# Eight of sixteen layer norms moved from VectorE to GpSimd in a linear-attention block

## The chip, the cores and the metric

The kernel runs on one core of a Trainium2 chip. The metric is the time on the device in microseconds (us). Each kernel is executed several times, and one execution is recorded by the hardware profiler; durations, waits and idle times come from that one.

## What is computed

The input x has 2048 tokens of 640 features in bf16. Each token is normalised (layer norm without weights), and the result xn feeds two branches whose product is added to x.

```python
xn = (x - mean(x)) / sqrt(var(x) + 1e-5)
q, k, v = split(xn @ wqkv)                # 32 heads of 20
phi = lambda t: where(t > 0, t + 1, exp(t)) + 1e-6
kv  = phi(k)^T v                          # per head, over all 2048 tokens
z   = sum over tokens of phi(k)
s   = (phi(q) kv / (phi(q) z + 1e-6)) @ wo
g   = silu(relu(xn @ w1) @ w2)            # w1: 640 x 1728, w2: 1728 x 640
out = x + s * g
```

## The kernel before

The 2048 tokens are 16 token tiles of 128 (tile t; tokens on the 128 partitions, 640 columns), in four chunks j of 512 tokens. Most products are done as pairs of chunks or tiles in a seven-product scheme in place of eight (the units a, b, p, q, m, u, o, g with steps s1 to s7): some products of a unit take sums or differences of operands, which VectorE forms in SBUF, and VectorE and ScalarE combine and evacuate the PSUM banks.

**Layer norm of a tile.** `LN_stats(t)` gives VectorE two BATCH_NORM_STATS (L630) and one BATCH_NORM_AGGREGATE (L634), then GpSimd two one-column instructions: L636 adds epsilon to the variance (`rsv`), L638 raises it to the power -0.5 (`rsy`), the reciprocal deviation. `LN_norm(t)` (L649) is one instruction on 128 x 640 bf16 that subtracts the mean and multiplies by `rsy`, both per-partition scalars, and writes `xn`. Behind it `xnT_dma(t)` (L698) issues on SP a transposing DMA from `xn` to `xnT`, which TensorE reads. Tiles 0 to 3 also have a short way at the start, in which only the mean is taken off first.

**What reads it.** The high tiles, 8 to 15, are read transposed by the K halves (`K_mm`, L709; Ka9 is the first 320 columns of tile 9, Kb8 the second of tile 8), by hh1 = `H_half(1)` (narrow matmuls, L817, all of tiles 8 to 15; hh0 in front of it takes tiles 0 to 7), by T1 = `h_T` (VectorE subtractions for the b units), and by the units themselves (L1198). The sum over tokens of phi(k) is done by accumulating DMAs issued by GpSimd (`z_put`, L897, words y0 to y15); the first of each of its two chains waits for the transposes of all tiles 8 to 15.

**What sets the order.** A class `Sched` records every operation with its reads and writes. `PROGRAM` is a text of words written out by hand (n8 is statistics and norm of tile 8, in which the statistics of tile 8 have been done earlier; the others up to n15 do both). TensorE and SP run their operations in the order in which they were recorded. VectorE, ScalarE and GpSimd are reordered after the first part (`end_of_head`): `place` plays the program with costs from `cost`, and for each of these engines picks among the next 60 operations the one that can start first, with ties going to the one that is due first (`late`, counted back from TensorE's queue). Waits on semaphores are then put in by `emit`. Each engine executes its own list strictly in order.

On SP the norms' transposes stand in the order n8, n9, n11, n10, n14, n12, n15, n13, with loads of x and w1 between them. In `PROGRAM` the part around the last two is

```
... n12 p1.s3 n15 p1.s4 p0.s1 Ka8 p0.s5 a0.s5 p0.s6 a0.s1 p0.s2 Kb11 a0.s6 p0.s7 p0.s3 n13
Ka10 Ka11 a0.s3 p0.s4 a0.s7 a0.s2 Kb9 Ka14 a3.s1 a0.s4 a2.s5 Kb12 a3.s5 a3.s6 a2.s1 hh0 hh1 ...
```

Other lines that matter: L735 and L737 finish phi(k) on VectorE (`K_fin`), L782 and L970 finish phi(q) (`f_sum`); L970 is the helper `tt` for all two-input adds and subtractions of VectorE, with both inputs in SBUF or one in PSUM; L1082 (`scale_rows`) is a GpSimd cast of 128 x 512; L1482 is ScalarE's evacuation of a K half.

Of the kernel before, what the change touches and what calls it, by code (L numbers as in the profile page):

```python
# [4 lines left out]
ALU = mybir.AluOpType  # L5
# [27 lines left out]
def _cols(ap):  # L33
    n = 1
    for d in ap.shape[1:]:
        n *= d
    return n


def _wide(ap):  # L40
    return str(ap.dtype).endswith("float32")


def cost(E, fn):
    seen = _Seen()
    fn(seen)
    name, a, k = seen.call
    aps = [v for v in list(a) + list(k.values()) if hasattr(v, "shape") and hasattr(v, "dtype")]
    if E == "PE":
        if name == "transpose":  # L50
            return (0.107, 0.107) if a[1].offset % a[1].ap[0][0] < 640 else (0.056, 0.107)
        n = _cols(k["rhs"]) / 2400.0
        part = k["lhsT"].shape[-1] / 128.0 if k.get("tile_position") is not None else 1.0
        return max(n * part + 0.0025, 0.026), n
    n = max(_cols(v) for v in aps)
    if E == "ACT":
        more = 0.19 if k.get("accum_out") is not None else 0.0
        if n > 512:
            more += 0.02
        if n == 1 and k["func"] == ACTF.Silu:  # L60
            more += 1.3
        if hasattr(k.get("scale"), "shape"):
            more += 0.08
        if _wide(k["out"]) and _wide(k["in_"]) and k["out"].tensor.name == k["in_"].tensor.name:
            return 0.05 + 0.0009 * n, 0.17 + 0.00083 * n
        return 0.05 + 0.00083 * n + more, 0.17 + 0.00083 * n + more
    if E == "POOL":
        return (0.66, 0.66) if k.get("op") is ALU.pow else (0.33 + 0.0025 * n, 0.33 + 0.0025 * n) if n > 12 else (0.33, 0.33)
    out = k["out"] if "out" in k else a[0]
    wide = any(_wide(v) for v in aps if _cols(v) > 4)  # L70
    if name == "bn_stats":
        return 0.403, 0.478
    if n <= 12:
        return 0.13, 0.21
    if name == "reciprocal":
        return 0.815, 0.9
    if name in ("tensor_copy", "tensor_scalar", "memset"):
        more = 0.06 * sum(hasattr(k.get(q), "shape") for q in ("scalar1", "scalar2"))
        return (0.065 + 0.00105 * n, 0.15 + 0.00105 * n) if wide else (0.08 + 0.00024 * n + more, 0.16 + 0.00025 * n + more)
    if wide or name != "tensor_tensor":  # L80
        return 0.064 + 0.00105 * n, 0.155 + 0.00105 * n
    return 0.075 + 0.000515 * n, 0.148 + 0.00052 * n
# [12 lines left out]
class Sched:  # L95
# [44 lines left out]
    def _record(self, E, kind, fns, R, W, extra, sem=None):  # L140
# [5 lines left out]
        if kind == "dma":  # L146
            seen = _Seen()
            fns[0](seen)
            name, a, _k = seen.call
            o.turn = "transpose" in name  # L150
            o.occ = 1.3 if o.turn else 1.25 if E == "POOL" else 0.5
            fat = a[1].tensor.name
            if fat in ("in_A_wo_dram", "reg3") and E == "SP" and not o.turn:
                o.occ = 0.65
            size = 2.0
            for d in a[0].shape:
                size *= d
            names = [v.tensor.name for v in a[0:2]]
            o.byt = 0.6 if o.turn else size / {"scr": 205e3}.get(names[0], {"scr": 240e3}.get(names[1], 310e3))
            lag = 0.5 if names[1] == "scr" else 0.8 if names[1] == "reg3" and names[0] == "reg6" else 0.0  # L160
            if o.turn and names[0] == "wv_sb":
                o.byt = 2.0
            o.dur = 4.6 if E == "POOL" else 2.1 + o.byt if o.turn else 1.95 + o.byt + lag
        else:
            o.occ, o.dur = 0.0, 0.0
            o.turn = E == "PE" and any(_narrow(fn) for fn in fns)
            for fn in fns:
                occ, dur = cost(E, fn)
                o.dur = o.occ + dur
                o.occ += occ  # L170
# [178 lines left out]
def bass_recurrent_scan__linear_attn_block__dense_activation_relu__prompt_kernel(  # L349
# [159 lines left out]
    sc = Sched(nc, NDS)  # L509
# [20 lines left out]
    def xs(t):  # L530
        return t if t < XR else (t - 4) % XR
# [112 lines left out]
        aggr(t)  # L644

    norms = []

    def LN_norm(t):
        norms.append(sc.op("DVE", lambda eng: eng.tensor_scalar(  # L649
            out=xn[:, t, :], in0=xin[:, xs(t), :], scalar1=mv[:, t, 0:1], scalar2=rsy[:, t:t + 1],  # L650
            op0=ALU.subtract, op1=ALU.mult), R=[("xin", xs(t)), ("mv", t), ("rsy", t)], W=[("xn", t)]))
        xnT_dma(t)
# [44 lines left out]
    def xnT_dma(t):  # L697
        dma("SP", lambda eng: eng.dma_start_transpose(  # L698
            xnT[:, t // 4, :, P * (t % 4):P * (t % 4 + 1)], xn[:, t, :]), R=[("xn", t)], W=[("xnT", t)])
# [667 lines left out]
    def run(ops):  # L1367
        for op_ in ops:
            op_[0](*op_[1:])

    S, N, F, SH, ZS, T0 = LN_stats, LN_norm, K_fin, h_S, scale_h, h_T
    after = [[(S, 5), (N, 4)], [(S, 6), (N, 5)], [(S, 7), (N, 6)], [(F, 0), (N, 7)], [(F, 1)]]
    for n, f in enumerate(HP):
# [576 lines left out]
```

## Time and profile before

| | |
|---|---|
| median of 3 runs | 203.54 us (203.54 to 203.79) |
| the profiled execution | 203.94 us, of which 202.7 us are the span from first to last instruction |
| busy, share of the span | TensorE 98%, VectorE 85%, ScalarE 63%, GpSimd 18% |
| chain that ended last | PE 82%, DMA 11%, issue 3%, DVE 3% |
| GpSimd L636 (1 column) x16 | 4.1 us, mean 259 ns |
| GpSimd L638 (1 column) x16 | 9.7 us, mean 608 ns |
| VectorE L649 (640 columns) x16 | 393 to 447 ns |

In the profile TensorE is PE (its weight loads PEld), VectorE is DVE, ScalarE ACT, GpSimd POOL, SyncE SP. A digit of the slices is the busy share of a fortieth of the span in tenths. In a timeline a row gives start, duration, engine, line, operation, output <- input, shapes and count, and in brackets how long the engine had been idle in front of it and what released it. Consecutive instructions of VectorE and ScalarE overlap by some 0.1 us in the records, so that the distance of starts is less than the duration.

### The profile page before, as it was taken

The page shows a single profiled execution, that of the slowest core. Times are in us where ns is not written, and L with a number is a line of the kernel's source. Part 1 is how long each engine was busy: PE and PEld are TensorE (multiplying, and loading weights), DVE is VectorE, ACT ScalarE, POOL GpSimd, SP SyncE. Part 2 cuts the span into 40 slices and gives each one's busy share as a digit, 9 for nine tenths or more (in the row PEclk, how much of TensorE's full clock was granted, in tenths as well). Part 3 has the DMA queues.
Part 4 walks back from the last instruction along what each step waited for, and adds up shares of the span by engine and source line. Part 5 has one row for each costly group of instructions (what it writes and reads, how often), then busy time and mean ns, then how long its engine had stood idle before and what let it go on. Part 6 is the DMA issues. An engine that isn't in the chain of part 4 may idle for free.

```text
span 202.7 us, 3677 instructions
## 1 busy us (share of the span) xinstructions
PE 198.6 (98%) x1334; PEld 123.8 (61%) x1344; DVE 172.2 (85%) x404; ACT 128.5 (63%) x268; POOL 37.2 (18%) x66
## 2 busy tenths in 40 slices
PE   8999999999999999999999999999999999999995
PEld 7755644545444454445645778777777777777773
DVE  4898999999997678899988879999978896855765
ACT  6497959799988486999662132463544645563452
POOL 3183051332256436422200000000000000000000
DMA  6976995662359858963462799338961106106103
GB/s 194 330 210 126 261 205 111 141 143 44 68 131 178 172 108 162 226 129 65 96 167 56 241 293 315 117 98 256 366 209 65 66 32 165 65 26 173 65 16 113
DMA packets 38328, 30.43 MB, mean 150 GB/s; under 512 B 13478, under 2 KB 38310, under 8 KB 38310
## 3 DMA queue, kind: packets, MB, share of 16 engines
q1 hardware_dynamic: 32437, 23.24, 41.0%
q0 software_dynamic: 4624, 5.57, 14.0%
q10 hardware_dynamic: 1248, 1.39, 2.1%
q8 instruction: 10, 0.16, 0.3%
q14 instruction: 9, 0.07, 0.1%
HBM read 15.81 MB, written 5.24 MB: 104 GB/s over the span
## 4 chain that ended last, share of the span: by engine, by line
PE 82%; DMA 11%; issue 3%; DVE 3%; ACT 0%; POOLq 0%; DVEq 0%
PE psT L1025 42%; PE psT L1198 18%; PE psT L709 10%; DMA regH<-reg 6%; PE psT L799 5%; DMA regH<-regH 3%; DMA reg<-in_A_x_dram 1%; PE psT L817 1%; PE psT L761 1%; PE psT L1826 1%; PE psT L682 1%; PE psT L1621 1%; PE psT L1595 1%; DVE regH L970 1%; PE psT L929 1%
## 5 line engine op out<-in xcount | busy, mean ns | idle before, releaser
L1198 PE MATMUL psT<-reg 128*128 128x512 bf16 (+1 forms) x135 | 36.8, 379 | 0.5 <-DVE regH L970 0.2
L1025 PE MATMUL psT<-reg,regH 128*128 128x320 bf16 (+1 forms) x224 | 35.0, 299 | 0.0
L1025 PE MATMUL psT<-reg 128*128 128x320 bf16 (+1 forms) x178 | 28.6, 299 | 0.0
L1025 PEld LDWEIGHTS psT<-reg,regH 128*128 128x128 bf16 (+1 forms) x224 | 21.9, 98 | 8.5
L1198 PEld LDWEIGHTS psT<-reg 128*128 128x128 bf16 (+1 forms) x141 | 13.4, 98 | 16.6 <-DVE regH L970 1.1
L897 POOL DMA_DIRECT2D regH<-reg x16 | 18.4, 1206 | 24.7 <-DMA regH<-reg 8.7
L1032 ACT ACTIVATE reg<-psT 128x320 f32<-128x320 f32 (+1 forms) x24 | 10.4, 435 | 17.8 <-PE psT L1025 15.9
L1025 PEld LDWEIGHTS psT<-reg 128*128 128x128 f16 (+1 forms) x178 | 17.4, 98 | 6.9
L970 DVE TENSOR_TENSOR reg<-reg 128x1024 f16<-128x1024 bf16 (+9 forms) x28 | 18.7, 673 | 1.1 <-PE psT L1025 1.0
L709 PE MATMUL psT<-reg 128*128 128x320 bf16 x120 | 18.7, 299 | 0.0
L1248 ACT ACTIVATE regH<-psT 128x512 bf16<-128x512 f32 (+1 forms) x24 | 15.2, 644 | 2.5 <-PE psT L1198 2.1
L1025 PE MATMUL psT<-reg,pqT 128*128 128x320 bf16 (+1 forms) x84 | 16.6, 299 | 0.0
L970 DVE TENSOR_TENSOR psT<-psT,reg 128x320 f32<-128x320 f32 (+1 forms) x21 | 11.4, 543 | 5.7 <-PE psT L1025 3.9
L1652 ACT ACTIVATE wv_sb<-psT 128x320 bf16<-128x320 f32 x22 | 9.6, 437 | 10.3 <-PE psT L1025 10.2
L709 PEld LDWEIGHTS psT<-reg 128*128 128x128 bf16 x120 | 11.7, 98 | 7.0
L1482 ACT ACTIVATE regE<-psT 128x320 bf16<-128x320 f32 x32 | 13.8, 538 | 2.9 <-PE psT L709 2.8
L630 DVE BATCH_NORM_STATS2 stats<-reg 128x6 f32<-128x320 bf16 x32 | 14.1, 473 | 1.3 <-DMA reg<-in_A_x_dram 1.3
L1032 ACT ACTIVATE psT<-psT 128x320 f32<-128x320 f32 x17 | 7.2, 426 | 10.3 <-PE psT L1025 10.3
L970 DVE TENSOR_TENSOR reg<-psT,reg 128x320 bf16<-128x320 f32 (+2 forms) x17 | 8.4, 499 | 4.2 <-PE psT L1025 4.1
L1841 ACT ACTIVATE reg<-psT 128x640 bf16<-128x640 f32 (+1 forms) x14 | 7.9, 569 | 5.1 <-PE psT L1025 5.1
L778 ACT ACTIVATE pqT<-psT 128x512 bf16<-128x512 f32 x16 | 10.6, 669 | 0.0
L776 ACT ACTIVATE regE<-psT 128x512 bf16<-128x512 f32 x16 | 10.1, 664 | 0.7 <-PE psT L761 0.5
(164 smaller groups left out, 385.5 us busy)
## 6 DMA issues: line engine op xcount, KB each, us to landing
regH<-reg POOLq DMA_DIRECT2D x16, 320.0 KB, 3.8
reg<-in_B_w_dram SPq DMA_DIRECT2D x12, 320.0 KB, 4.7
scr<-rden SPq DMA_DIRECT2D x4, 640.0 KB, 6.2
reg<-in_A_x_dram SPq DMA_DIRECT2D x4, 640.0 KB, 8.8
out_dram<-reg SPq DMA_DIRECT2D x14, 160.0 KB, 1.8
regE<-scr SPq DMA_DIRECT2D x3, 640.0 KB, 4.7
reg<-in_A_x_dram SPq DMA_DIRECT2D x4, 320.0 KB, 3.5
reg<-in_A_wo_dram SPq DMA_DIRECT2D x6, 160.0 KB, 5.2
```

The source lines that it names most:

```text
L630: sc.op("DVE", lambda eng: eng.bn_stats(stats[:, t, a, :], xv[:, HN * a:HN * (a + 1)]), R=[("xin", xs(t))], W=[("stats", t, a)])
L709: fns.append(lambda eng, a=a, k=k, lhs=lhs: eng.matmul(ps[bk[a]][:, 0:HN], lhsT=lhs, rhs=wk[:, k, HN * a:HN * (a + 1)], start=(k == 0), st ...
L776: exps.append(sc.op("ACT", lambda eng: eng.activation(out=e_, in_=src, func=ACTF.Exp), R=[key], W=[("er_e", es)]))
L778: sc.op("ACT", lambda eng: eng.activation(out=pqT[:, f, schunk(j)], in_=src, func=ACTF.Relu), R=[key], W=[("pqT", j, f)], extra=hz(gone))
L799: sc.group("PE", [(lambda eng, k=k: eng.matmul(ps[b], lhsT=w1_col(k, P * f, P), rhs=src[:, k, :], start=(k == 0), stop=(k == C - 1))) for ...
L897: dma("POOL", lambda eng: eng.dma_start(zacc[a], src, **kw), R=[key] + after, W=[("zacc", a)], chain=zchain[a])
L970: sc.op("DVE", lambda eng: eng.tensor_tensor(out=out, in0=in0, in1=in1, op=op), R=R, W=W, extra=extra)
L1025: sc.group("PE", [(lambda eng, k=k, lhs=lhs, rhs=rhs: eng.matmul(ps[b][:, 0:HN], lhsT=lhs, rhs=rhs, start=(start and k == 0), stop=(k == n ...
L1032: sc.op("ACT", lambda eng: eng.activation(out=dst, in_=ps[b][:, 0:HN], func=ACTF.Copy), R=[("ps", b)], W=[dkey], extra=extra)
L1198: sc.group("PE", [(lambda eng, k=k, lhs=lhs, rhs=rhs: eng.matmul(ps[b][:, 0:nn], lhsT=lhs if tile is None else rhs, rhs=rhs if tile is Non ...
L1248: sc.op("ACT", lambda eng: eng.activation(out=dst, in_=ps[b], func=ACTF.Relu), R=[("ps", b)], W=[("hT", j, f)], extra=ex)
L1482: sc.op("ACT", lambda eng, func=func, slot=slot: eng.activation(out=ek[:, eks(t), slot, HN * a:HN * (a + 1)], in_=ps[b][:, 0:HN], func=fun ...
```

## The change

The norms of tiles 8 to 15 are given to GpSimd, where their `rsv` and `rsy` are also done. The planner's cost of a GpSimd instruction with more than 12 columns is set from 0.33 + 0.0025 n to 0.33 + 0.0016 n us. PROGRAM, and with it the orders of TensorE and SP, stay; the orders of VectorE, ScalarE and GpSimd are worked out anew by `place`.

```diff
     if E == "POOL":
-        return (0.66, 0.66) if k.get("op") is ALU.pow else (0.33 + 0.0025 * n, 0.33 + 0.0025 * n) if n > 12 else (0.33, 0.33)
+        return (0.66, 0.66) if k.get("op") is ALU.pow else (0.33 + 0.0016 * n, 0.33 + 0.0016 * n) if n > 12 else (0.33, 0.33)
...
     norms = []
+    NP = range(8, 16)
 
     def LN_norm(t):
-        norms.append(sc.op("DVE", lambda eng: eng.tensor_scalar(
+        norms.append(sc.op("POOL" if t in NP else "DVE", lambda eng: eng.tensor_scalar(
             out=xn[:, t, :], in0=xin[:, xs(t), :], scalar1=mv[:, t, 0:1], scalar2=rsy[:, t:t + 1],
             op0=ALU.subtract, op1=ALU.mult), R=[("xin", xs(t)), ("mv", t), ("rsy", t)], W=[("xn", t)]))
         xnT_dma(t)
```

## The prediction

> **What bounds the kernel now.** I read the page first (busy shares, the 40 slices, the chain), then the stretches from 24 us on, then the line of the norms, and last the timeline in order of time around the GpSimd work and around the last norm.
>
> ```profile
> PE 198.6 (98%) x1334; PEld 123.8 (61%) x1344; DVE 172.2 (85%) x404; ACT 128.5 (63%) x268; POOL 37.2 (18%) x66
> ...
> DVE  4898999999997678899988879999978896855765
> ACT  6497959799988486999662132463544645563452
> POOL 3183051332256436422200000000000000000000
> ```
>
> TensorE has work in 98% of the span, so the end is set by its queue, which is in a fixed order, and by whatever makes that queue wait. The stretches show how dense it is where the eight norms lie (their VectorE starts are 26.82 to 51.34 us):
>
> ```profile
> 24.00:34.00 10.00, 10.00 (x49) 4.65 (x49) 9.54 (x25) 7.70 (x15) 4.23 (x11) 1.00 0.87 176
> 34.00:44.00 10.00, 9.95 (x53) 4.98 (x53) 9.69 (x29) 8.75 (x20) 3.24 (x8) 1.00 0.69 149
> 44.00:54.00 10.00, 9.95 (x56) 5.42 (x56) 9.99 (x31) 10.00 (x26) 1.64 (x4) 1.00 0.33 65
> 54.00:64.00 10.00, 9.89 (x77) 4.53 (x78) 9.72 (x27) 8.64 (x18) 5.09 (x5) 1.00 0.64 134
> ```
>
> After the length come TensorE, weight loads, VectorE, ScalarE, GpSimd, clock, DMA. From 24 to 64 us TensorE idles 0.21 us, from 24 to 200 us 0.61 us (175.39 busy of 176). A 512-column matmul is recorded 0.38 us long but the next starts 0.216 us later, so short gaps are hidden; by the spacing of the starts I count about 1.0 us of waiting in all after 24 us (the largest 0.34 us at 104 us). The granted clock is 1.00 throughout. VectorE is full too from 24 to 64 us, but TensorE hardly waits for it: its results come early enough. So a VectorE relief can win about 1 us at the very most, and a new wait of TensorE is lost in full, because nothing behind it has slack to give back.
>
> **What is removed: 8 norms on VectorE.**
>
> ```profile
> L649 DVE TENSOR_SCALAR reg<-reg,mv,rsy x16: 393/434/447, 13.4 to 51.3; 128x640 bf16<-128x640 bf16 x16
> ```
>
> Recorded 0.43 us, but pipelined: 31.59 to the next start 31.94 is 0.35 us. Eight of them give back 8 x 0.35 = 2.8 us of VectorE between 26.8 and 51.8 us. By itself this is worth nothing on TensorE, whose waits there sum to 0.2 us.
>
> **What is added: 8 norms on GpSimd.** No GpSimd row has 640 columns. The nearest ones: the same kind of instruction on one column (L636) takes 0.22 us; affine_select on 160 columns (L606) 0.35; the cast L1082 on 512 columns 0.85. From one column to the cast is (0.85 - 0.22) / 511 = 1.23 ns a column, so 640 columns come to 0.22 + 0.79 = 1.0 us. But look at what stood beside that cast:
>
> ```profile
> 25.41 0.32 DVE L735 TENSOR_SCALAR regE<-regE 128x640 bf16<-128x640 bf16 x1
> 25.76 0.49 DVE L737 TENSOR_TENSOR reg<-regE 128x640 bf16<-128x640 bf16 x1
> 25.87 0.85 POOL L1082 CAST spx<-rsy 128x512 f16<-128x512 f32 x1
> 26.17 0.73 DVE L735 TENSOR_SCALAR regE<-regE 128x640 bf16<-128x640 bf16 x1
> ```
>
> The cast ends at 26.72 and the VectorE instruction caught beside it ends at 26.90: 0.73 us for what takes 0.32 us just before. Ahead of it L737 runs to 26.25, so the cast may have waited too and own only 26.25 to 26.72 = 0.47 us. The lower end for a norm is then 0.47 x 640/512 = 0.6 us; the upper, as it does two operations with two per-partition scalars, 0.22 + 2 x 0.79 = 1.8 us. I take 1.05 us, nearest to the cast as recorded. So a norm is 0.7 us slower than on VectorE, and there is a second price: VectorE is held while it runs.
>
> The Trainium skill, page "SBUF — State Buffer", section "Who interferes with whom", says that GpSimd and VectorE share one port pair as an exclusive lock, taken for a whole instruction, against VectorE instructions in a two-port mode or with two SBUF inputs. It speaks against this change, and the row above (0.73 against 0.32 us) agrees. The page "GPSIMD Engine Reference", section "3.1 Elementwise — side-by-side cycle accounting", gives 1.03 cycles an element for bodies of up to two operations; at its 1.2 GHz that is an estimate of 0.55 us for 640 elements ahead of dispatch, by which the sum below would be no stall at all; no run here shows it yet.
>
> What does holding VectorE cost? The only pair the trace shows held is a bf16 tensor_scalar beside the cast. Bounds per norm: nothing, or the whole 1.05 us. Statistics (L630, 7.1 us between 24 and 54 us), aggregates (1.6) and adds with a PSUM operand (2.7 + 1.4 + 1.4) have nothing of this seen; they are 14.2 of the 31.9 us of recorded VectorE time there without the norms, 45%. I take the other 55%: 0.55 x 1.05 = 0.58 us lost a norm, against 0.35 saved, net 0.23 us later a norm. Six norms stand ahead of the two last: 1.4 us later, of which the two VectorE waits at 33.7 and 42.6 us (0.39 + 0.21) swallow 0.6. So VectorE stands about 0.8 us later at 49 us, with -2.1 us (nothing held) and +3.6 us (wholly held: 6 x 0.70 - 0.6) as ends. Against that, the planner, which knows the longer norm, sees each norm's statistics due earlier by its own 1.35 in place of 0.39 us (0.33 + 0.0016 x 640 against 0.16 + 0.00025 x 640 + 0.12 by the code's formulas for their durations: 0.9 us) and may pull them forward in VectorE's order by that much. I let the two cancel.
>
> **Where it meets the path.** Each norm releases a transposing DMA on SP, in fixed order n8 n9 n11 n10 n14 n12 n15 n13, and that releases TensorE work. For the first six the cover is enough. L638 of tile 9 ends at 31.41, so the norm ends at 32.5 instead of 32.02: its DMA lands 2.7 us later (the median), 35.2, and Ka9 starts at 36.50. Tile 11: 38.53 + 1.05 = 39.6 (39.14 before), landing 42.3, Kb11 at 43.25: 0.9 us left. Tile 10: 41.6 (41.22), landing 44.3, Ka10 at 45.66. Tiles 14 and 12 come no later than now (43.4 against 43.89; 45.4 against 46.91). Tile 8, behind the cast on GpSimd's queue, ends at 27.8 rather than 27.25, and Kb8 starts at 32.37. If GpSimd took 1.8 us, tiles 11 and 10 would use their cover up. The last two are different:
>
> ```profile
> 49.22 0.28 POOL L636 TENSOR_SCALAR rsv<-mv 128x1 f32<-128x1 f32 x1 [5.86 <-DVE mv L634]
> 49.58 0.57 POOL L638 TENSOR_TENSOR rsy<-rsv,mhalf 128x1 f32<-128x1 f32 x1
> 50.22 0.22 POOL L636 TENSOR_SCALAR rsv<-mv 128x1 f32<-128x1 f32 x1
> 50.25 0.43 DVE L649 TENSOR_SCALAR reg<-reg,mv,rsy 128x640 bf16<-128x640 bf16 x1
> 50.53 0.58 POOL L638 TENSOR_TENSOR rsy<-rsv,mhalf 128x1 f32<-128x1 f32 x1
> 51.34 0.44 DVE L649 TENSOR_SCALAR reg<-reg,mv,rsy 128x640 bf16<-128x640 bf16 x1
> 54.54 1.69 PE L817 MATMUL psT<-reg 128*32 128x512 bf16 x28
> 54.90 1.69 POOL L897 DMA_DIRECT2D regH<-reg  x2 [3.80 <-DMA reg<-reg]
> ```
>
> Today the norms of tiles 15 and 13 follow one another closely and the last ends at 51.78; the accumulating DMA of L897, which waits for all eight high tiles, is let go at 54.90, so the last transpose has landed there. The narrow matmuls of L817 start at 54.54 and are 40 at 0.057 us, up to 56.82: the second 20 (hh1), from 55.68, need tile 13. Cover: 0.8 us. After the change both norms stand in one GpSimd queue with tile 13's L636 and L638: 50.15 + 0.9 (the pair, start to end 50.22 to 51.11) + 2 x 1.05 + 0.15 for a wait on VectorE = 53.3, which is 1.5 us later than 51.78. TensorE then waits 1.5 - 0.8 = 0.7 us at hh1, with everything behind it. In that wait lie VectorE's own delays: T1's first subtraction (54.88) is released by the same landing, and the PSUM add at 55.48, done 56.1, is needed by a3.s7 at 57.26. The z chain of GpSimd DMAs starts later as well, but its last part hangs on the K tiles of 75 us, which move with TensorE. I add 0.1 us for small waits elsewhere, as ScalarE is also full (10.00 of 10 us).
>
> **Sum.** The profiled execution took 203.94 us (span 202.7); with +0.8 us, 204.7. It stands 0.4 us above the median of the three runs, 203.54, so the forecast on that scale is 204.3 us.
>
> **The rivals.**
> - No stall (20%). GpSimd needs only 0.6 to 0.7 us: 50.15 + 0.9 + 1.3 = 52.35, 0.6 us later than 51.78 and inside the 0.8 us. For it: the cast's possible 0.47 us. Against: the lock that would explain that also delays VectorE. Decides: a norm under 0.7 us. Time 203.5.
> - VectorE falls behind (20%). The norms hold it wholly: at 1.35 us each, 6 x 1.0 - 0.6 = 5.4 us late at most; half of that, less the 0.9 us pull, is 1.8 us on the last statistics, and the norms end 50.15 + 0.9 + 2.7 - 51.78 = 2.0 us later: 1.8 + 2.0 - 0.8 = 3.0 us, 206.5; with half of that drift (0.9 us) 205.6, and with none 204.7. For it: 0.73 against 0.32. Against: the 45% of VectorE's work that was not seen held.
> - Faster (10%). VectorE's 2.8 us are not taken back by holding, its statistics and TensorE's inputs come up to 2 us earlier, and the replanned order removes most of the 1.0 us of waits; this begins where a norm costs VectorE under 0.35 us. Price: -0.5 us, 203.0. Against: the larger waits lie at 78 to 104 us, behind the z chain and other work, and not at the norms.
>
> **How the numbers follow.** My forecast, the wait at hh1, gets 50%, own range 203.8 to 205.0. The range 203.2 to 205.9 reaches down over "no stall" and part of "faster", and up over the milder part of the hold; it leaves out about 2 in 10. Some 0.2% (0.41 us) is what a measurement of this kernel can tell from no change. Slower by more: 0.68 (nearly all of the forecast, all of the hold); within: 0.22 (the no-stall case and an edge of the forecast); faster by more: 0.10.
>
> **What would show it.** Right: L649 on GpSimd at about 1 us; VectorE tensor_scalar and two-input rows beside it at 0.7 us or more; the last norm ending near 53.3; a TensorE gap of some 0.7 us inside L817 around 56 us, and no other new one over 0.2 us. Wrong: a norm under 0.7 us or over 1.4; L817 running through; new gaps at the K tiles (L709) of 43 to 46 us; or statistics placed so much earlier that the last norm ends before 52.5 us.

## The result and the profile after

The changed kernel takes 212.78 us (median of four, 212.32 to 213.02) against 203.56 us beside it: a ratio of 1.0448, 95% interval 1.0427 to 1.0468, 9.2 us slower. The forecast was 204.3 us with 205.9 as its upper end. Disturbed runs are left out of every ratio here; of the kernel "truecost" below they leave only two of four runs, and so no ratio.

The profiled execution took 212.32 us, span 211.1 (before 203.94 and 202.7). The page shows a hole (line numbers behind 647 are one higher than before, so L649 is now L650):

```profile
PE 200.9 (95%) x1334; PEld 123.4 (58%) x1344; DVE 170.4 (81%) x396; ACT 128.7 (61%) x268; POOL 61.8 (29%) x74
...
PE   8999999999629999999999999999999999999995
...
DVE  5998998999129458789998977999988887855855
...
POOL 3272398999945561651220000000000000000000
PEclk9999999999966999999999999999999999999999
...
PE 70%; POOL 13%; DVE 8%; DMA 5%; issue 2%; ACT 0%
```

GpSimd is full from 26 to 59 us, TensorE and VectorE are empty around 58 us, and behind that the granted clock falls to 6 tenths for two slices. In the chain GpSimd now has 13% (before, none). The group of the norms, by engine, gives the reason:

```profile
L650 DVE TENSOR_SCALAR reg<-reg,mv,rsy x8: 394/441/447, 12.9 to 20.9; 128x640 bf16<-128x640 bf16 x8
L650 POOL TENSOR_SCALAR reg<-reg,mv,rsy x8: 2511/2603/3142, 26.3 to 56.6; 128x640 bf16<-128x640 bf16 x8
```

A norm takes 2.5 to 3.1 us on GpSimd, not 1.05. The timeline around the last two:

```profile
47.07 3.09 POOL L650 TENSOR_SCALAR reg<-reg,mv,rsy 128x640 bf16<-128x640 bf16 x1
50.35 0.20 POOL L636 TENSOR_SCALAR rsv<-mv 128x1 f32<-128x1 f32 x1
50.52 1.02 POOL L638 TENSOR_TENSOR rsy<-rsv,mhalf 128x1 f32<-128x1 f32 x1
51.06 3.03 POOL L638 TENSOR_TENSOR rsy<-rsv,mhalf 128x1 f32<-128x1 f32 x1
54.10 2.51 POOL L650 TENSOR_SCALAR reg<-reg,mv,rsy 128x640 bf16<-128x640 bf16 x1
56.60 2.51 POOL L650 TENSOR_SCALAR reg<-reg,mv,rsy 128x640 bf16<-128x640 bf16 x1
...
54.88 1.26 PE L818 MATMUL psT<-reg 128*32 128x512 bf16 x20
62.05 2.32 PE L818 MATMUL psT<-reg 128*32 128x512 bf16 x20 [5.92 <-DMA reg<-reg]
...
61.99 1.29 DVE L971 TENSOR_TENSOR reg<-reg 128x1024 f16<-128x1024 bf16 x2 [8.30 <-DMA reg<-reg]
```

The last norm ends at 59.1 (before 51.78; forecast 53.3). Its transpose is issued at 59.14 and lands at about 62.0, and both hh1 on TensorE and T1 on VectorE have waited for it. The stretches show the clock beside the hole:

```profile
44.00:54.00 10.00, 9.95 (x56) 5.35 (x56) 9.64 (x29) 10.00 (x25) 9.81 (x8) 1.00 0.18 36
54.00:64.00 10.00, 4.03 (x44) 1.36 (x43) 2.01 (x4) 3.37 (x8) 6.80 (x5) 0.79 0.24 43
64.00:74.00 10.00, 9.95 (x45) 4.31 (x43) 6.98 (x19) 6.94 (x14) 5.26 (x4) 0.87 0.80 162
```

**The account of the span, +8.4 us.** hh0 starts 0.34 us later (54.88 against 54.54). The wait at hh1 is 56.02 to 62.05, 6.03 us by the spacing of the starts (the bracket of its row, which counts from the recorded end, says 5.92). hh1's 20 matmuls take 2.26 us to the next start in place of 1.14: +1.12. The next nine 512-column matmuls (the profile holds eight of them) take 64.31 to 67.39, 3.08 us against 1.95 (56.82 to 58.77): +1.13. Sum 8.6; 0.2 us come back later, where TensorE waited 0.34 us at 104 us before and 0.12 at the same place (113 us) now.

### The profile page after: what moved, and what is told of

Read it like the earlier page. It is cut to its first block, busy times and chain, and to the rows that moved or that the text cites. A ratio compares the mean times of both kernels' runs of the same rounds, so it can differ in the third digit from the quotient of the medians.

```text
span 211.1 us, 3679 instructions
## 1 busy us (share of the span) xinstructions
PE 200.9 (95%) x1334; PEld 123.4 (58%) x1344; DVE 170.4 (81%) x396; ACT 128.7 (61%) x268; POOL 61.8 (29%) x74
## 3 DMA queue, kind: packets, MB, share of 16 engines
q10 hardware_dynamic: 1248, 1.39, 2.0%
## 4 chain that ended last, share of the span: by engine, by line
PE 70%; POOL 13%; DVE 8%; DMA 5%; issue 2%; ACT 0%
PE psT L1026 41%; PE psT L1199 20%; POOL reg L650 8%; DMA reg<-reg 4%; POOL rsy L638 4%; DVE stats L630 3%; PE psT L710 3%; PE psT L1497 2%; DMA reg<-in_A_x_dram 1%; PE psT L818 1%; DVE reg L650 1%; POOL rsv L636 1%; PE psT L1827 1%; DVE mv L634 1%; PE psT L1622 1%
## 5 line engine op out<-in xcount | busy, mean ns | idle before, releaser
L898 POOL DMA_DIRECT2D regH<-reg x16 | 18.9, 1244 | 24.9 <-DMA regH<-reg 9.3
L1199 PEld LDWEIGHTS psT<-reg 128*128 128x128 bf16 (+1 forms) x141 | 13.5, 99 | 16.9 <-issue 1.0
L650 POOL TENSOR_SCALAR reg<-reg,mv,rsy 128x640 bf16<-128x640 bf16 x8 | 21.7, 2714 | 0.4
L1483 ACT ACTIVATE regE<-psT 128x320 bf16<-128x320 f32 x32 | 13.5, 537 | 3.4 <-PE psT L710 3.3
L638 POOL TENSOR_TENSOR rsy<-rsv,mhalf 128x1 f32<-128x1 f32 x16 | 12.3, 801 | 1.1
```

The source lines that it names most:

```text
L638: sc.op("POOL", lambda eng: eng.tensor_tensor(out=rsy[:, t:t + 1], in0=rsv[:, t:t + 1], in1=mhalf[:, :], op=ALU.pow), R=[("rsv", t), ("mha ...
L650: norms.append(sc.op("POOL" if t in NP else "DVE", lambda eng: eng.tensor_scalar(out=xn[:, t, :], in0=xin[:, xs(t), :], scalar1=mv[:, t, 0 ...
L898: dma("POOL", lambda eng: eng.dma_start(zacc[a], src, **kw), R=[key] + after, W=[("zacc", a)], chain=zchain[a])
L1199: sc.group("PE", [(lambda eng, k=k, lhs=lhs, rhs=rhs: eng.matmul(ps[b][:, 0:nn], lhsT=lhs if tile is None else rhs, rhs=rhs if tile is Non ...
L1483: sc.op("ACT", lambda eng, func=func, slot=slot: eng.activation(out=ek[:, eks(t), slot, HN * a:HN * (a + 1)], in_=ps[b][:, 0:HN], func=fun ...
```

## The experiments

Theory Q: the norm is slow by itself on GpSimd, and eight of them with their L636 and L638 form a queue that ends late. Its rivals: H, a norm holds VectorE; H2, VectorE holds GpSimd; and that only the planner's order is at fault. The new planner cost alone leaves the order of every engine as it was, so it was not run by itself. The edits are given shortened, in part in words.

### forms: GpSimd instructions by themselves

The edit replaces the block by instructions on constants:

```diff
+    norm()                                   # 640 columns, two scalars, subtract and multiply
+    tensor_scalar(320 columns, two scalars)  # L399
+    tensor_scalar(one scalar, subtract)      # L400
+    tensor_scalar(two immediates)            # L401
+    tensor_scalar(f32, two scalars)          # L402
+    tensor_copy; tensor_tensor(multiply)     # L403, L404
```

> A kernel that leaves the whole block out and only times instructions on constants: GpSimd forms with VectorE idle (three times each), then VectorE streams alone (8) and beside three norms and three L636/L638 pairs on GpSimd. Theory Q (the norm is slow by itself): the 640-column norm takes 2.5 us with VectorE idle, as the last two norms of the changed kernel did; whether this comes from the two per-partition scalars, the two operations or the bf16 type is open: if from the operations, one operation takes about half (1.3 us) and immediates change nothing; if from the scalars, immediates take about 1 us; if from bf16, the f32 form takes about 1 us. 320 columns about 1.3 us. Theory H (holding): beside tensor_scalar and two-input streams VectorE instructions are stretched to a norm's length, 2.5 us, at least once for each norm. Rival H2 (the reverse): VectorE rows keep their length and GpSimd waits: norms beside those streams take 3 us or more and the small L638 3 us in place of 0.57, while beside bn_stats and adds from PSUM they stay at 2.5 and 0.57.

The groups of this kernel's GpSimd instructions (line, form, count, busy us, mean ns; the 15 norms hold 12 beside VectorE streams):

```profile
L377 POOL TENSOR_SCALAR pout<-pin,mean,one 128x640 bf16<-128x640 bf16 x15 | 38.7, 2581 | 6.8 <-DVE psT L369 5.9
L402 POOL TENSOR_SCALAR fout<-fin,mean,one 128x640 f32<-128x640 f32 x3 | 7.5, 2498 | 0.0
L401 POOL TENSOR_SCALAR pout<-pin 128x640 bf16<-128x640 bf16 x3 | 7.1, 2354 | 0.3
L400 POOL TENSOR_SCALAR pout<-pin,mean 128x640 bf16<-128x640 bf16 x3 | 5.7, 1884 | 0.3
L399 POOL TENSOR_SCALAR pout<-pin,mean,one 128x320 bf16<-128x320 bf16 x3 | 4.3, 1437 | 0.3
L404 POOL TENSOR_TENSOR pout<-pin 128x640 bf16<-128x640 bf16 x3 | 4.2, 1391 | 0.3
L403 POOL COPY pout<-pin 128x640 bf16<-128x640 bf16 x3 | 2.1, 717 | 0.0
```

With VectorE idle a norm took 2.51 to 2.52 us: Q holds. The bf16 type is not the reason (f32 2.50), nor are the scalars (immediates 2.35). Tensor_scalar itself is slow: 1.88 us with one operation, while a copy takes 0.72 and even a two-input multiply 1.39. From 320 to 640 columns it is (2.51 - 1.43) / 320 = 3.4 ns a column. The planner's 0.33 + 0.0016 x 640 = 1.35 us fits the multiply, not the norm. Beside VectorE streams in which each instruction waits for the one ahead, three norms took 8.36 us (tensor_scalar), 8.16 (adds), 7.73 (bn_stats) and 7.73 (adds from PSUM), and L638's like 0.57 to 0.78: neither H nor H2 in the form expected.

### stream and nowait: denser VectorE streams

```diff
-    each VectorE instruction writes the same output
+    ten outputs in turn (stream); runs of 50, 30, 40 or 30 instructions without a wait (nowait)
```

> Again a kernel without the block, on constants. VectorE instructions write ten buffers in turn, so that none waits for the one ahead: streams of 4x tensor_scalar, of two-input adds, of both in turn, and of bn_stats; beside each, GpSimd runs two L636/L638 pairs, two norms and one pair. Theory H2 (a dense VectorE stream starves GpSimd, the reason that the two L638 at 50.5 us of the changed kernel took 3.57 us in place of 1.14): L638 takes 2 us or more, or ends only with the stream, beside tensor_scalar, adds or the mix, and 0.57 beside bn_stats. Rival (it was something else, such as other traffic): 0.57 to 0.8 us everywhere, as in the run before in which each VectorE instruction waited for the one ahead.

> Once more without the block, on constants: the same VectorE streams, now as runs of 50 tensor_scalar, 30 adds, 20 of both in turn and 30 bn_stats with no wait on a semaphore between them, beside two L636/L638 pairs, two norms and a pair on GpSimd. Theory H2b (what starves GpSimd is a run of VectorE instructions without a wait between them): the first pair is held until the run of tensor_scalar or of both in turn ends, 10 us or more, and bn_stats hold nothing. Rival: L638 takes 0.6 to 0.9 us and a norm 3.1 to 3.4 us as in the streams with waits, and the 3.03 us of the changed kernel stay unexplained.

Beside the tensor_scalar stream of "stream":

```profile
8.50 0.59 POOL L380 TENSOR_SCALAR dev<-one 128x1 f32<-128x1 f32 x1
9.17 0.86 POOL L381 TENSOR_TENSOR dev<-one,mhalf 128x1 f32<-128x1 f32 x1
11.60 6.16 POOL L377 TENSOR_SCALAR pout<-pin,mean,one 128x640 bf16<-128x640 bf16 x2
```

and its stretches of VectorE, beside the two norms and afterwards alone:

```profile
11.60:17.70 6.10, 6.10 (x19) 1.00 0.00 1
20.00:33.00 13.00, 13.00 (x57) 1.00 0.00 0
```

A norm takes 3.1 us there (3.4 beside adds, 2.6 beside bn_stats), and VectorE goes on: 6.10 / 19 = 0.32 us an instruction against 13.0 / 57 = 0.23 (two-input adds: 6.70 / 15 = 0.45 against 13.5 / 35 = 0.39). So both lose some, and neither waits for the other's whole instruction. "nowait" gave the same: L638's like 0.66 to 0.92, two norms 6.15 us. H falls. The 3.03 us of L638 did not come up in either: H2b falls, and the rival named there holds. (H2 and H2b fall for constant streams; "calm" comes back to the stream of the kernel itself.)

### calm: the changed kernel with VectorE stopped beside L638

```diff
+        # the first L783 at 50.8 us also waits for the L638 of tile 13
+        dve[at + 15].deps.add(rsy_13)
```

> The changed kernel, all orders the same, with one wait more: VectorE's instruction that starts at 50.82 us (the first of three L783) waits until GpSimd's L638 of tile 13 has ended. Theory H2 (VectorE's run of instructions with SBUF operands from 50.8 to 53.7 us holds that L638 for 3.03 us): the two L638 take 0.57 to 0.7 us each, the last norm ends 2.3 us earlier, near 56.8 us, VectorE makes up its 1 us while it waits for the transposes anyway, and hh1 waits 3.7 in place of 6.0 us: 210.4 us, less if the clock falls less. Rival (the 3.03 us has another cause in GpSimd): L638 again 3 us, and the time 212.8 us or more.

Measured 210.71 us, ratio 1.0320 (1.0274 to 1.0365), 2.1 us less than the change. L638, L650 and L818 are L646, L660 and L828 there:

```profile
50.98 1.07 POOL L646 TENSOR_TENSOR rsy<-rsv,mhalf 128x1 f32<-128x1 f32 x2
52.06 5.72 POOL L660 TENSOR_SCALAR reg<-reg,mv,rsy 128x640 bf16<-128x640 bf16 x2
...
55.33 1.26 PE L828 MATMUL psT<-reg 128*32 128x512 bf16 x20
60.52 2.33 PE L828 MATMUL psT<-reg 128*32 128x512 bf16 x20 [3.93 <-DMA reg<-reg]
```

The two L638 take 1.07 us in place of 3.57, and the wait shrinks by 2 us. That VectorE's instructions held that L638 is shown for this order: only VectorE's start was moved. In other orders the two L638 are not held, though VectorE works beside them (1.36 us for both in "last2", 1.47 in "truecost"). Which property of the stream does it is open, since constant streams hold one for 0.9 us at most.

### fill: TensorE kept busy while it waits

```diff
-        "hh1": lambda: H_half(1, take()),
+        "hh1": 26 matmuls of 512 columns on data that is there, then H_half(1, take())
```

> The changed kernel with 26 matmuls of 512 columns, on data that is there, put ahead of the matmuls of hh1 (results overwritten). Orders of all engines are otherwise those of the changed kernel. Theory: the wait at hh1 is 6.0 us for the landing of tile 13 and does not shrink, but the granted clock stays 1.00 behind it; the 1.1 us that hh1 and the 1.2 us that the next eight 512-column matmuls lost come back: 210.4 us. Rival: the low clock has nothing to do with the idle time before it: 212.8 us, clock again 0.8 in the ten us after.

211.46 us, ratio 1.0364 (1.0338 to 1.0390): 1.3 us less than the change, not 2.4. The granted clock was 1.000 in all four runs, where the change had 0.984 in its four.

```profile
56.30 5.79 PE L1529 MATMUL psT<-reg,const-bfloat16-1.0 128*128 128x512 bf16 x26
62.20 1.26 PE L818 MATMUL psT<-reg 128*32 128x512 bf16 x20
63.40 0.60 PE L1199 MATMUL psT<-regX,rden 128*128 128x512 f16 x2
65.28 0.60 PE L1199 MATMUL psT<-regX,reg 128*128 128x512 f16 x2 [1.28 <-DVE psT L971]
```

hh1 is back at 1.20 us, but then a3.s7 waits for VectorE's add from PSUM, which stands behind T1, released by the same landing. The low clock had partly covered that wait. The profiled execution is the slowest of the four (212.65 us), and it has another wait that neither the change nor the kernel before has in this length, 1.03 us by the starts:

```profile
113.30 0.61 PE L1199 MATMUL psT<-reg 128*128 128x512 f16 x2 [0.87 <-DVE regH L971]
```

So the clock is shown to follow the idle time, but of the 2.2 us that it cost, about one was not won back.

### n13, last2, n14, first4, six: which norms cost

```diff
-    NP = range(8, 16)
+    NP = (13, )      # n13;    (13, 15) last2;    (14, ) n14
+    NP = (8, 9, 10, 11)      # first4;    (8, 9, 10, 11, 12, 14) six
```

> The change for tile 13 alone. Theory Q: only the norm's own length counts, 51.1 + 2.5 = 53.6 us against 51.78, less the 0.8 us of cover: hh1 waits 1.0 us, 204.6 us. Theory H2: VectorE's dense stream at 51 to 55 us delays the norm or its L638 by up to 2.5 us more: 206 to 207 us. If the whole loss of the change were in other norms: 203.5 us.

> The change for tiles 13 and 15 alone. Theory Q: both norms stand behind one another, 51.1 + 2 x 2.5 = 56.1 us for the last, landing 58.8, hh1 (due at 55.7) waits 3.1 us: 206.7 us; with a starved L638 up to 209. If the queue that the six norms ahead build up were needed for any loss: below 204.5 us.

> The change for tile 14 alone, which has 3.7 us between landing and use. Theory Q: 42.3 + 2.5 = 44.9 us against 43.9, covered; tile 12's L636 and L638 wait behind it and end at 45.8, also covered: 203.5 us, within 0.4. Theory that giving back VectorE time is worth something by itself: below 203.2 us. Theory that a GpSimd norm costs VectorE its length: above 204 us.

> The change for tiles 8 to 11 alone. Theory Q: four norms of 2.5 us have ended by 42.2 us; tile 9 comes 0.3 us too late for Ka9 as in the changed kernel, tile 10 within its cover, and the statistics of 14, 12, 15 and 13 are served as before: 203.6 + 0.3 = 203.9 us, up to 204.5. If every norm on GpSimd cost its share of the 9.2 us: 208 us.

> The change without tiles 15 and 13, whose norms stay on VectorE. Theory Q: GpSimd's queue still ends its sixth norm at 50.2 us, then the pairs of 15 and 13 follow; if VectorE's dense stream there starves them as in the changed kernel, they end at 54.1, the norms on VectorE at 54.9, landing 57.8, hh1 waits about 2 us: 205.6 to 206 us. If the pairs are not starved, they end at 52 and the norms at 52.9: hh1 waits 0.4 us, 204.2 us. If the loss hung on the K tiles of the first six norms: above 207 us.

| kernel | median us | ratio to before | longest TensorE wait in the profile, by the starts |
|---|---|---|---|
| n14 | 203.78 | 0.9998 (0.9986 to 1.0010) | none near the norms |
| first4 | 204.89 | 1.0060 (1.0036 to 1.0083) | 0.54 us, at 36.5 us (Ka9) |
| n13 | 205.51 | 1.0079 (1.0061 to 1.0097) | 1.70 us, hh1 |
| six | 206.42 | 1.0133 (1.0107 to 1.0159) | 2.41 us, at 51.7 us |
| last2 | 208.71 | 1.0237 (1.0179 to 1.0295) | 3.56 us, hh1 |

n14 shows two things: a norm of 2.52 us with 3.7 us of cover costs nothing, and giving back VectorE's time for one norm (0.35 us) gains nothing. Relief of VectorE by all eight, without their cost, was not run. n13 costs more than the 1.0 us expected, since the planner put its norm in front of tile 15's L636 (51.91) and L638 (52.27), so that tile 15, whose transpose goes first on SP, came late too. last2 loses 5 us with two norms alone, without a queue of six ahead of them; its four runs are 207.44 us at a granted clock of 1.000, 208.61 and 208.80 at 0.992, 210.41 (the profiled one) at 0.984, so the time rises as the clock falls, by up to 3 us if the clock alone makes the spread. In six the time came out near what was expected, but not where:

```profile
54.15 0.60 PE L1199 MATMUL psT<-regE,reg 128*128 128x512 f16 x2 [2.24 <-DVE regH L971]
```

The two norms left on VectorE wait for their L638 behind GpSimd's sixth norm (50.06), and VectorE's add for TensorE is queued behind them; L818 then runs through at 57.31. Its two L638 took 1.08 us, with VectorE waiting. first4 is 1 us above what was expected; its profiled run (204.28 us) shows only the 0.54 us at Ka9, the others reach 206.29, and where they lose it is open.

### split and truecost: a shorter norm, a better plan

```diff
+    # split: GpSimd normalises columns 0:320 of tiles 8 to 15, VectorE 320:640
+    # truecost: planner's GpSimd cost 0.33 + 0.0036 * n
```

> The change with GpSimd doing columns 0 to 319 of the eight norms (1.43 us by the run of forms) and VectorE columns 320 to 639; nothing left out. Theory Q: the chain of eight is 8 x (1.43 + 0.9) = 18.7 us in place of 27, so that the statistics and not GpSimd's queue set the pace again; the last two norms end near 50.15 + 0.9 + 2.9 = 53.9 us, hh1 waits 1.3 us: 204.9 us, up to 206.5 if the pairs are starved. If the loss came from the sharing with VectorE and not from the length of the norm, it would be nearly that of the change: above 209 us.

> The changed kernel with the planner's cost of a GpSimd instruction set to 0.33 + 0.0036 n, 2.63 us for a norm, near the measured 2.5; only orders change. Theory Q: the queue of eight norms of 2.5 us and eight pairs is as long as before, hh1 waits 4 to 6 us: 210.5 to 212.5 us. Rival (a wrong order, from a planner that holds the norm for 1.35 us, makes most of the loss): below 207 us.

split: 205.59 us, ratio 1.0098 (1.0069 to 1.0126); its half norms take 1.45 to 1.99 us, and hh1 waits 1.47 us at full clock. GpSimd has as many instructions as in the change, only shorter ones, and 7 of the 9 us are gone: the length of the norm on GpSimd is what counts. truecost: 210.80 and 211.25 us, too few runs for a ratio. The last norm ends at 57.7, and hh1 waits 3.92 us, but 0.63 and 1.37 us are lost at 35 and 37 us. By these two runs the order is worth 1.5 to 2 us, not the loss, and part of that is the L638 that is not held in it. No kernel here is faster than the one before.

## Why the prediction was wrong

- **What bounds the kernel: right.** A new wait of TensorE was lost nearly in full (8.4 of 8.6 us), and relief of VectorE by one norm brought nothing (n14).
- **The price of the norm: the step that failed.** It was read off a cast's slope, 1.05 us with 0.6 and 1.8 as ends. Measured: 2.51 alone, up to 3.14. A cast is a poor neighbour for a tensor_scalar with two operations: a copy of the same 640 columns is 0.72 us. In the sum the last two norms were 2 x 1.05 + 0.15 = 2.25 us and took 5.02. The page "GPSIMD Engine Reference" of the Trainium skill, section "3.1 Elementwise — side-by-side cycle accounting", whose 1.03 cycles an element had given the estimate of 0.55 us, was further off.
- **The queue and the held L638: left out.** I took the norms of the first six tiles to start at the L638 times of before. At 2.5 + 0.9 us or more each, GpSimd had one pause from 26 to 59 us (0.56 us at 34.3 us), so L638 of the last tiles waited for the sixth norm (to 50.12 us) rather than for statistics, and the last norm came 7.3 us late, not 1.5. The statistics of the last tile were done at 50.14 us before; now those of the last two are done at 45.11:

```profile
49.94 0.20 DVE L634 BATCH_NORM_AGGREGATE mv<-stats 128x2 f32<-128x12 f32 x1
44.84 0.27 DVE L634 BATCH_NORM_AGGREGATE mv<-stats 128x2 f32<-128x12 f32 x2
```

The first row is from the kernel before, the second from the change. I let VectorE's hold and the planner's pull of 0.9 us cancel; in fact the statistics came 5 us earlier, and the queue used that up. (By the terms given there, the planner's duration of a VectorE norm is 0.44 us, not 0.39; the 0.9 us stand.) That GpSimd came to the last pairs at 50.12 us, where the forecast had 50.15, is therefore luck. The 5.8 us from the forecast 53.3 to 59.1 lie behind that point: 2.8 us are the length of the last two norms, 2.5 us the held L638 (3.57 against 1.07 us in "calm"), and about 0.6 us the pair of tile 15, which the forecast had as done by then. The queue of the first six norms is not needed for most of the loss (last2 loses 5 us without it); alone it costs 2.7 us (six).
- **The place: right.** Tile 13, hh1, cover 0.8 us, T1 in the shadow of the same landing. The wait there was priced at 0.7 us and measured 6.03. Tile 9 used its cover up as well (0.46 us at Ka9 by the starts).
- **Holding: one side was missed.** I priced VectorE's loss at 0.58 us a norm and none for GpSimd beyond 0.15 us in all. In the runs on constants VectorE lost (0.32 - 0.23) / 0.32 x 3.1 = 0.9 us a norm beside its densest stream and near nothing beside bn_stats; in the kernel that loss did not reach the path. GpSimd lost up to 0.6 us on norms (0.9 beside adds on constants) and 2.5 us on the two L638, the latter right on the path. The page "SBUF — State Buffer" of the Trainium skill, section "Who interferes with whom", has the loser wait for a whole instruction; here 19 VectorE instructions went by during two norms, and 15 adds with both inputs in SBUF, so it does not describe these pairs.
- **The clock: not considered.** Some 2.2 us of TensorE at reduced speed followed the six idle us, of which keeping TensorE busy gave back 1.3. The clock fell 3.8 us into the wait here, 2.4 us into that of last2, and stayed at 1.00 in n13 (wait 1.70 us). The page "TensorE: Matmul & The Clock Gate" of the Trainium skill, section "Part 1: The HAM clock gate (the "warmup" mystery)", says that the clock halves after an idle window of about 3.4 us and needs as long of steady work to come back; the traces agree in the main, but not with the 2.4 us. I priced waits without it.
- **The rivals.** "VectorE falls behind" had the sign and, at 206.5 us, the nearest number, by the wrong mechanism: VectorE's statistics came earlier, not later. "No stall" falls with the norm of 2.51 us, "faster" with the time.

## What to carry to other kernels

Before moving an instruction to another engine, find a row of the same operation at the same size on that engine, or measure it by itself; a cast or a copy says little about tensor_scalar. Where the moved work sits in one queue with the small instructions that release it, price the queue too (here 2.5 + 0.9 = 3.4 us or more for each tile; between the start of tile 8's L636 at 24.95 us and the end of tile 13's L638 at 51.1 us of the kernel before there are 3.3 for each of the eight), and above all the last pieces in it, on which the path waits. Move only what has cover, and then ask what the relief is worth: where TensorE is full, nothing.

## What was not expected of the hardware

- GpSimd's tensor_scalar on 128 x 640 takes 1.88 us with one operation and 2.51 with two, its two-input multiply 1.39, its copy 0.72 (bf16, VectorE idle, "forms").
- A one-column GpSimd instruction of 0.57 us took 3.03 us beside VectorE work in the change, and about 0.53 with VectorE stopped ("calm").
- In waits of TensorE of 3.6 to 6.0 us the granted clock in the profile fell to 0.50, for 6.8 us (the change, calm, last2) or 3.4 us (truecost), and hh1's matmuls took 0.113 in place of 0.057 us. In waits of 1.5 to 2.4 us (split, n13, six) it stayed at 1.00, and in last2, with 3.6 us in its profile, it differed from run to run (1.000, 0.992, 0.992, 0.984).
